# Attention and MLP on one core: both dense layers in seven products, shared PSUM bank pairs, a list that places every operation

## The chip, the cores and the metric

The kernel runs on one core of one Trainium2 chip. The metric is the device time in microseconds (us); lower is better. The core has a matrix engine (TensorE, PE in the profile, with PEld for its weight loads), VectorE (DVE), ScalarE (ACT), GpSimd (POOL) and SyncE (SP), which only starts transfers. Each engine works through its own queue in order; semaphores make one wait for another. Matmuls write to PSUM, eight banks of 512 fp32 values per partition.

## The reference

```python
scores = q @ k^T / sqrt(64)              # q, k, v: 8 batches x 12 heads x 448 x 64
attn   = maximum(scores, 0)**2 / 448
x      = heads of (attn @ v) side by side    # 3584 tokens x 768
h      = x @ w_in                        # 768 x 2048
g      = h * sigmoid(1.702 * h)
out    = g @ w_out                       # 2048 x 768
```

Inputs and output are fp32.

## The kernel before

**Units of attention.** Four heads of one batch are a unit, 24 in all. Its k and q are loaded, cast to fp16 and transposed: units 0 to 5 on PE (`trans_pe`, L138, with a copy on DVE, L142), the others by transposing transfers on SP's queue (`trans`, L111). A slot `s` is one seventh of a unit's scores: four 64x64 matmuls (L159) into a pair of PSUM banks, a ReLU on ACT (L175) or DVE (L173), and a square `x` on DVE (L447) into an `at` tile. When seven slots are squared, `a` multiplies them with v (28 matmuls, L190), and `xt_evac` (L210, L213) moves the result to a tile of x, transposed, with tokens in the free dimension.

**Groups of tokens.** The tokens are cut into eight groups of 384 and 512 in turn. Layer one, `m1` (L238): for each of 16 blocks of 128 hidden features, six matmuls of the whole group into one bank, GELU on ACT to an fp32 tile `gf` (L243), and a scaling ("widening") to fp16 on POOL into `gt` (L245). Layer two for group 0 and one odd piece: `m2` (L264), 16 matmuls per 128 tokens and half of the outputs.

**Seven products in layer two.** For the other groups, two 128-token pieces, two halves of the hidden features and two halves of the outputs form 2x2 blocks, and `pair` (L303) computes seven products of eight matmuls in place of eight. Sums of `gt` (L298) and of `w_out` (L288) are made on DVE. Each product has its own bank; DVE adds it, times 1/SC, to one or two places of the output tile `osb` (L314), after two of them were copied to `ea` and `eb` on ACT (L312). A piece without a partner goes through `single` (L389). Finished tiles are stored on SP's queue (L255); the last product of all is split into two halves of 192 columns with a store each.

**PSUM.** `ps_s` holds three pairs of banks for scores and attention results, `ps_m` two single banks for layers one and two.

**What sets the order.** A list of words, written out by hand or by a planner, is executed in order (`for w in words`). Each engine receives its instructions in the order of the words. A slot's ReLU is issued with its matmuls, or, with the letter h, after the next word of the dense layers (`release`). A few zero matmuls (`z`) and doubled slots (letter t) keep PE at work near the start.

Of the kernel before, what the change touches and what calls it, by code (L numbers as in the profile page):

```python
# [15 lines left out]
def kernel(  # L16
# [15 lines left out]
    NU = B * NP  # L32
    NK = DM // 128
    NF = DFF // 128
    NOUT = DM // 2
    SC = float(D * S)
    WQ = 4
    WO = 8

# [3 lines left out]
    for n in gblk:  # L43
# [3 lines left out]
    cst = ctx.enter_context(tc.tile_pool(name="cst", bufs=1))  # L47
    stp = ctx.enter_context(tc.tile_pool(name="stp", bufs=2))
    c16 = ctx.enter_context(tc.tile_pool(name="c16", bufs=3))
    v16p = ctx.enter_context(tc.tile_pool(name="v16p", bufs=5))  # L50
    qkT = ctx.enter_context(tc.tile_pool(name="qkT", bufs=3))
    rlp = ctx.enter_context(tc.tile_pool(name="rlp", bufs=3))
    atp = ctx.enter_context(tc.tile_pool(name="atp", bufs=11))
    xtp = ctx.enter_context(tc.tile_pool(name="xtp", bufs=3))
    gfp = ctx.enter_context(tc.tile_pool(name="gfp", bufs=3))
    gtp = ctx.enter_context(tc.tile_pool(name="gtp", bufs=1))
    smp = ctx.enter_context(tc.tile_pool(name="smp", bufs=1))
    osp = ctx.enter_context(tc.tile_pool(name="osp", bufs=3))
    ps_s = ctx.enter_context(tc.tile_pool(name="ps_s", bufs=3, space=bass.MemoryType.PSUM))
    ps_m = ctx.enter_context(tc.tile_pool(name="ps_m", bufs=2, space=bass.MemoryType.PSUM))  # L60

    ident = cst.tile([128, 128], F16, name="ident")
    gate = cst.tile([1, 64], F16, name="gate")
    warm = cst.tile([1, 1], F32, name="warm")
    win = [cst.tile([128, NK, WQ * 128], F16, name=f"win{i}") for i in range(NF // WQ)]
    wout = [[cst.tile([128, WO, NOUT], F16, name=f"wout{h}_{i}") for i in range(NF // WO)]
            for h in range(2)]

    wsum = [cst.tile([128, WO, NOUT], F16, name=f"wsum{i}") for i in range(3)]


    units = {}

    def quad(t, b, pr):
        return t[b].rearrange("(a i s) (p j) d -> i (s p) a (j d)", a=2, i=NP, j=J)[pr]

    def load_qk(u):
        b, pr = divmod(u, NP)
        st = units.setdefault(u, {})
        for n, t in (("k", k), ("q", q)):  # L80
            x = stp.tile([128, 2, S], F32, name=f"{n}st", tag=f"{n}st")
            nc.sync.dma_start(
                out=x,
                in_=quad(t, b, pr))
            st[n] = x

    def load_v(u):
        b, pr = divmod(u, NP)
        st = units.setdefault(u, {})
        x = v16p.tile([128, 2, S], F16, name="v16", tag="v16")  # L90
        nc.gpsimd.dma_start(
            out=x,
            in_=quad(v, b, pr))
        st["v16"] = x

    def cast(u, n, eng):
        st = units[u]
        c = c16.tile([128, J, 2, D], F16, name=f"{n}16", tag=f"{n}16")
        o = c.rearrange("p j a d -> p a j d")
        i = st[n].rearrange("p a (j d) -> p a j d", d=D)  # L100
        if eng is nc.scalar:
            eng.activation(out=o, in_=i, func=AF.Copy)
        else:
            eng.tensor_copy(out=o, in_=i)  # L104
        st[n + "16"] = c

    def trans(u):
        st = units[u]
        for n in ("k", "q"):
            t = qkT.tile([128, J, 128], F16, name=f"{n}T", tag=f"{n}T")  # L110
            nc.sync.dma_start_transpose(  # L111
                out=t[:, :, :], in_=st[n + "16"].rearrange("p j a d -> p (j a d)"))
            st[n + "T"] = t

    def load16(u, n):
        b, pr = divmod(u, NP)
        st = units.setdefault(u, {})
        x = c16.tile([128, 2, J, D], F16, name=f"{n}16", tag=f"{n}16")
        nc.gpsimd.dma_start(
            out=x,  # L120
            in_=quad({"k": k, "q": q}[n], b, pr))
        st[n + "16"] = x

    def cast16(u, n, eng):
        c = c16.tile([128, 2, J, D], F16, name=f"{n}16", tag=f"{n}16")
        o, i = c.rearrange("p a j d -> p a (j d)"), units[u][n]
        if eng is nc.scalar:
            eng.activation(out=o, in_=i, func=AF.Copy)
        else:
            eng.tensor_copy(out=o, in_=i)  # L130
        units[u][n + "16"] = c

    def trans_pe(u, n):
        st = units[u]
        ps = ps_m.tile([128, 1024], F16, name="tr", tag="mm")
        for j in range(J):
            for a in range(2):
                nc.tensor.matmul(  # L138
                    out=ps[64 * a:64 * a + 64, j * 128:(j + 1) * 128],
                    lhsT=st[n + "16"][:, a, j, :], rhs=ident[:, :], is_transpose=True)  # L140
        t = qkT.tile([128, J, 128], F16, name=f"{n}T", tag=f"{n}T")
        nc.vector.tensor_copy(out=t, in_=ps[:, 0:J * 128])  # L142
        st[n + "T"] = t

    early = []

    def scores(u, j, times=1, banks=False):
        st = units[u]
        if early:
            sc = early.pop()  # L150
        elif banks:
            sc = [ps_m.tile([128, 512], F32, name="scm", tag="mm") for _ in range(2)]
        else:
            sc = ps_s.tile([128, 2, 512], F32, name="sc", tag="sc")
        for s in [0, 1] * times:
            for a in range(2):
                r = slice(64 * a, 64 * a + 64)
                c = slice(64 * s, 64 * s + 64)
                nc.tensor.matmul(  # L159
                    out=sc[a][c, 0:S] if isinstance(sc, list) else sc[c, a, 0:S],  # L160
                    lhsT=st["kT"][r, j, c],
                    rhs=st["qT"][r, :, c],
                    start=True, stop=True)
        return sc

    def relu2(u, j, sc, dve=False):
        rl = rlp.tile([128, 2, S], F16, name="rl", tag="rl")
        at = atp.tile([128, 2, S], F16, name="at", tag="at")
        halves = [(rl, sc[:, :, 0:S])] if not isinstance(sc, list) else [
            (rl[:, a, :], sc[a][:, 0:S]) for a in range(2)]  # L170
        for o, i in halves:
            if dve:
                nc.vector.tensor_scalar(out=o, in0=i, scalar1=0.0, scalar2=None, op0=ALU.max)  # L173
            else:
                nc.scalar.activation(out=o, in_=i, func=AF.Relu)  # L175
        pend[u, j] = (at, rl)
        return at

    pend = {}

    def av_mm(u, j, at):
        st = units[u]
        if "av" not in st:
            av = ps_s.tile([128, 2, 512], F32, name="av", tag="sc")
            st["av"] = [av[:, 0, :], av[:, 1, :]]
            st["pair"] = av
        for s in range(2):
            for a in range(2):
                r = slice(64 * s, 64 * s + 64)
                nc.tensor.matmul(  # L190
                    out=st["av"][s][64 * a:64 * a + 64, 0:S],
                    lhsT=st["v16"][r, a, 64 * j:64 * j + 64],
                    rhs=at[r, a, :],
                    start=(j == 0), stop=(j == J - 1))
# [3 lines left out]
    def xt_evac(u):  # L198
        b, pr = divmod(u, NP)
        st = units[u]  # L200
        lo = b * J
        while lo < (b + 1) * J:
            g = max(i for i in range(NG) if gcum[i] <= lo)
            hi = min((b + 1) * J, gcum[g + 1])
            if g not in xts:
                xts[g] = xtp.tile([128, NK, 512], F16, name="xt", tag="xt")
            c = slice(64 * (lo - gcum[g]), 64 * (hi - gcum[g]))
            f = slice(64 * (lo - b * J), 64 * (hi - b * J))
            if "pair" in st:
                nc.vector.tensor_copy(out=xts[g][:, 2 * pr:2 * pr + 2, c], in_=st["pair"][:, :, f])  # L210
            else:
                for s in range(2):
                    nc.vector.tensor_copy(out=xts[g][:, 2 * pr + s, c], in_=st["av"][s][:, f])  # L213
            lo = hi
        st.pop("pair", None)
        st.pop("av", None)

    ats = {}

    held = []  # L220

    def release():
        while held:
            u, j, sc = held.pop()
            ats[u, j] = relu2(u, j, sc)


    gts = {}

    def m1(g, f):  # L230
        n = 64 * gblk[g]
        if f == 0:
            gts[g] = gtp.tile([128, NF, 512], F16, name="gt", tag=f"gt{g % 2}")
# [24 lines left out]
    def m2(g, m, h):  # L258
# [13 lines left out]
        if h == 1:  # L272
            store(g, m, 0, DM, (nc.sync, nc.sync))
# [291 lines left out]
```

## Time and profile before

| | |
|---|---|
| median of 3 runs | 381.79 us (381.56 to 382.59) |
| span of the profiled execution | 380.2 us |
| PE busy | 369.7 us, 3136 matmuls |
| DVE busy | 256.8 us, 426 instructions |
| ACT busy | 215.7 us, 315 instructions |
| POOL busy | 133.2 us, 198 instructions |
| granted TensorE clock | 0.998 |

The profile is of one execution; its span, from the first to the last instruction, lies 1.6 us under the median of the runs. Busy is the time in which at least one instruction of the engine was under way. A row of the profile names the line, the engine, the operation, output and input tile with their shapes, a count, and then the busy time and the mean length of one; what follows is the idle time before these instructions and who ended it. Instructions of one engine can overlap by their start and end, so a length can exceed the distance from one start to the next.

### The profile page before, as it was taken

What the parts mean: (1) busy time and instruction counts of PE and PEld (TensorE: products, weight loads), DVE (VectorE), ACT (ScalarE), POOL (GpSimd) and SP (SyncE); (2) the same over time, 40 slices, a digit from 0 to 9 for tenths busy, and PEclk for the clock granted to TensorE, in tenths of its full rate; (3) what the DMA queues carried; (4) which work ended last, traced back from release to release, by engine and by line L of the source; (5) the groups of instructions that cost most, each with busy time, mean ns of one, the idle gap of its engine ahead of it and who ended that gap; (6) DMA issues with size and microseconds to landing.
All of it is one profiled execution on the core that took longest, in us unless ns stands there. A gap on an engine that the chain in (4) does not pass through costs nothing.

```text
span 380.2 us, 7870 instructions
## 1 busy us (share of the span) xinstructions
PE 369.7 (97%) x3136; PEld 194.1 (51%) x3136; DVE 256.8 (68%) x426; ACT 215.7 (57%) x315; POOL 133.2 (35%) x198
## 2 busy tenths in 40 slices
PE   7889999999999999999999999999999999999993
PEld 3455554544555555544455555544555555454552
DVE  3999843689869977577874995484348795032673
ACT  3988854567766845565877546386556643323110
POOL 7543644432363243143246132232631213313000
PEclk9999999999999999999999999999999999999999
DMA  8999998977775977789569656580292303010333
GB/s 179 203 205 205 203 282 187 213 198 155 216 158 93 197 177 127 148 242 141 91 230 177 132 100 129 156 153 3 46 149 34 84 2 84 2 41 0 85 83 84
DMA packets 65221, 51.30 MB, mean 135 GB/s; under 512 B 35744, under 2 KB 61728, under 8 KB 65184
## 3 DMA queue, kind: packets, MB, share of 16 engines
q1 hardware_dynamic: 48416, 36.61, 39.8%
q0 software_dynamic: 16608, 14.09, 26.0%
q8 instruction: 24, 0.39, 0.4%
q10 hardware_dynamic: 160, 0.10, 0.1%
q14 instruction: 13, 0.11, 0.1%
HBM read 45.61 MB, written 11.01 MB: 149 GB/s over the span
## 4 chain that ended last, share of the span: by engine, by line
PE 90%; DVE 6%; issue 1%; ACT 1%; ACTq 0%
PE ht L238 39%; PE op L303 29%; PE sc L159 9%; PE av L190 7%; PE op L264 4%; DVE at L447 2%; DVE osb L314 1%; PE zp L422 1%; ACT rl L175 1%; PE tr L138 1%; DVE kT L142 1%; DVE xt L213 1%; DVE qT L142 0%; DVE rl L173 0%; ACT eb L312 0%
## 5 line engine op out<-in xcount | busy, mean ns | idle before, releaser
L238 PE MATMUL ht<-xt,win 128*128 128x384 f16 (+1 forms) x768 | 156.2, 353 | 0.0
L245 POOL TENSOR_SCALAR gt<-gf 128x384 f16<-128x384 f32 (+1 forms) x128 | 81.5, 637 | 195.9 <-ACT gf L243 190.7
L175 ACT ACTIVATE rl<-sc 128x896 f16<-128x896 f32 x144 | 126.3, 918 | 33.8 <-PE sc L159 29.0
L243 ACT ACTIVATE gf<-ht 128x384 f32<-128x384 f32 (+1 forms) x128 | 69.9, 546 | 89.2 <-PE ht L238 75.3
L447 DVE TENSOR_TENSOR at<-rl 128x896 f16<-128x896 f16 x168 | 104.8, 656 | 14.8 <-ACT rl L175 13.9
L238 PEld LDWEIGHTS <-win 128*128 128x128 f16 x768 | 72.7, 98 | 73.1 <-issue 10.3
L303 PEld LDWEIGHTS <-gt 128*128 128x128 f16 x408 | 38.5, 98 | 30.0 <-issue 4.5
L159 PE MATMUL sc<-qT,kT 64*64 64x448 f16 x696 | 48.1, 357 | 1.5 <-ACT rl L175 0.8
L303 PEld LDWEIGHTS <-as 128*128 128x128 f16 x312 | 29.9, 98 | 22.7 <-issue 2.7
L303 PE MATMUL op<-wout,as 128*128 128x384 f16 x224 | 40.5, 326 | 0.0
L303 PE MATMUL op<-wsum,gt 128*128 128x384 f16 x224 | 40.1, 326 | 0.0
L314 DVE SCALAR_TENSOR_TENSOR osb<-op,osb 128x384 f32<-128x384 f32 (+1 forms) x45 | 23.6, 544 | 21.2 <-PE op L303 20.8
L190 PE MATMUL av<-at,v 64*64 64x448 f16 x616 | 33.2, 350 | 0.1
L303 PE MATMUL op<-wout,gt 128*128 128x384 f16 (+1 forms) x184 | 32.4, 319 | 0.5 <-DVE osb L314 0.5
L210 DVE CAST xt<-av 128x896 f16<-128x896 f32 (+2 forms) x32 | 24.6, 793 | 9.3 <-PE av L190 9.2
L159 PEld LDWEIGHTS <-kT 64*64 64x64 f16 x696 | 17.4, 105 | 25.3 <-issue 18.3
L173 DVE TENSOR_SCALAR rl<-sc 128x896 f16<-128x896 f32 x24 | 26.0, 1087 | 4.6 <-PE sc L159 4.5
L298 DVE TENSOR_TENSOR as<-gt 128x1024 f16<-128x1024 f16 x36 | 24.2, 699 | 6.7 <-POOL gt L245 6.7
L190 PEld LDWEIGHTS <-v 64*64 64x64 f16 x672 | 19.7, 107 | 13.4 <-issue 2.8
L104 POOL CAST q<-qst 128x896 f16<-128x896 f32 x18 | 17.1, 948 | 11.3 <-DMA qst<-in_q_dram 10.5
L314 DVE SCALAR_TENSOR_TENSOR osb<-op,ea 128x384 f32<-128x384 f32 x22 | 12.1, 552 | 12.1 <-PE op L303 6.0
L314 DVE SCALAR_TENSOR_TENSOR osb<-op,eb 128x384 f32<-128x384 f32 x22 | 12.1, 551 | 11.7 <-PE op L303 11.7
(40 smaller groups left out, 178.1 us busy)
## 6 DMA issues: line engine op xcount, KB each, us to landing
out_dram<-osb SPq DMA_DIRECT2D x54, 192.0 KB, 2.7
kst<-in_k_dram SPq DMA_DIRECT2D x19, 448.0 KB, 4.9
qst<-in_q_dram SPq DMA_DIRECT2D x19, 448.0 KB, 5.6
v<-in_v_dram POOLq DMA_DIRECT2D x24, 224.0 KB, 4.9
win<-in_moe_w_in_dram POOLq DMA_DIRECT2D x8, 384.0 KB, 12.3
wout<-in_moe_w_out_dram POOLq DMA_DIRECT2D x4, 768.0 KB, 10.7
k<-in_k_dram POOLq DMA_DIRECT2D x5, 224.0 KB, 8.8
q<-in_q_dram POOLq DMA_DIRECT2D x5, 224.0 KB, 9.1
```

The source lines that it names most:

```text
L159: nc.tensor.matmul(out=sc[a][c, 0:S] if isinstance(sc, list) else sc[c, a, 0:S], lhsT=st["kT"][r, j, c], rhs=st["qT"][r, :, c], start=True ...
L173: nc.vector.tensor_scalar(out=o, in0=i, scalar1=0.0, scalar2=None, op0=ALU.max)
L175: nc.scalar.activation(out=o, in_=i, func=AF.Relu)
L190: nc.tensor.matmul(out=st["av"][s][64 * a:64 * a + 64, 0:S], lhsT=st["v16"][r, a, 64 * j:64 * j + 64], rhs=at[r, a, :], start=(j == 0), st ...
L210: nc.vector.tensor_copy(out=xts[g][:, 2 * pr:2 * pr + 2, c], in_=st["pair"][:, :, f])
L238: nc.tensor.matmul(out=ht[:, 0:n], lhsT=w[:, kk, fo:fo + 128], rhs=xts[g][:, kk, 0:n], start=(kk == 0), stop=(kk == NK - 1))
L243: nc.scalar.activation(out=gf[:, 0:n], in_=ht[:, 0:n], func=AF.Gelu_apprx_sigmoid, scale=1.0 / SC)
L245: nc.gpsimd.tensor_scalar(out=gts[g][:, f, 0:n], in0=gf[:, 0:n], scalar1=SC, scalar2=1.0, op0=ALU.mult, op1=ALU.mult)
L298: nc.vector.tensor_tensor(out=out_, in0=x, in1=y, op=op)
L303: nc.tensor.matmul(out=op[:, 0:cw], lhsT=lhs[:, f, :], rhs=w[:, f, c0:c0 + cw], start=(start and f == 0), stop=(stop and f == HF - 1))
L314: nc.vector.scalar_tensor_tensor(out=o, in0=op[:, 0:w], scalar=sc, in1=add, op0=ALU.mult, op1=ALU.add)
L447: nc.vector.tensor_tensor(out=at, in0=rl, in1=rl, op=ALU.mult)
```

## The change

Layer one gets seven products too. For groups 1 to 7, four blocks of hidden features times two halves of the model dimension times two halves of the tokens form 2x2 blocks; four units of seven products replace 16 blocks of six matmuls. A product is six matmuls (three of the model dimension, two of the features) of half a group, 256 or 192 columns. Sums of x (`t_sum`) are made per group on DVE, sums of `w_in` (`s_sum`) once.

Both layers now use the form of seven products in which intermediate results are chained: products 0, 2, 4 and 5 accumulate in bank 0 of a pair, 1 in bank 1, then 3 and 6 in bank 1. Between them, bank 0 is copied out (a "snapshot", on ACT or DVE), and bank 1 is added to a snapshot on DVE. In layer one these are `unit_snap` (t) and `unit_add` (b) on fp32 tiles `gf`, followed by GELU (g) and widening (v); in layer two `pair_snap` (h) and `pair_last` (l) on the output tile.

PSUM is four pairs of banks, P0 to P3, used by all stages; the word names the pair (`@2`). Each operation is a word of its own: matmuls of a slot `s`, ReLU `r`, square `x`, transfer `e` of attention results, casts `K` and `Q`, transposing transfers `Rk` and `Rq`, loads `Lk` and `Lq`, products `u` and `p`. A letter after a colon names the engine (a ACT, d DVE, p POOL). 45 of the 168 squares are on POOL, and seven of the casts of later units on DVE. Staging tiles of k and q have one buffer each (two before), `at` eight (eleven before), `gf` five (three before). The doubled slots, the zero matmuls among the slots and the split of the last product are gone. Group 0 and the pieces without a partner keep eight products.

```diff
-    stp = ctx.enter_context(tc.tile_pool(name="stp", bufs=2))
...
-    ps_s = ctx.enter_context(tc.tile_pool(name="ps_s", bufs=3, space=bass.MemoryType.PSUM))
-    ps_m = ctx.enter_context(tc.tile_pool(name="ps_m", bufs=2, space=bass.MemoryType.PSUM))
+    for name, bufs in (("cst", 1), ("kst", 1), ("qst", 1), ("k16", 2), ("q16", 2), ("v16", 4),
+                       ("kT", 3), ("qT", 3), ("rl", 3), ("at", 8), ("xe", 1), ("xo", 2),
+                       ("T1", 1), ("T2", 1), ("T4", 1), ("ge", 1), ("go", 1), ("gf", 5),
+                       ("asm", 2), ("osb", 3)):
+        pool(name, bufs)
+    for i in range(4):
+        pool(f"P{i}", 1, space=bass.MemoryType.PSUM)
...
+    def square(e, p, u, j):
+        rl = slots[u, j]
+        at = new("at", [128, 2, S], F16)
+        tt(at, rl, rl, ALU.mult, e)
+        slots[u, j] = at
...
+    def s_sum(e, p, i, n):
+        s1, s2, s4 = winS[i]
+        a11, a12, a21, a22 = (w_in_block(i, f, h) for f in range(2) for h in range(2))
+        o, x, y, op = {1: (s1, a21, a22, ALU.add), 2: (s2, s1, a11, ALU.subtract),
+                       3: (a21, a21, a11, ALU.subtract), 4: (s4, a12, s2, ALU.subtract)}[n]
+        tt(o, x, y, op, e)
...
+    def t_sum(e, p, g, n):
+        b11, b12, b21, b22 = (x_block(g, h, t) for h in range(2) for t in range(2))
+        if n == 3:
+            tt(b12, b12, b22, ALU.subtract, e)
+            return
+        x, y = {1: lambda: (b12, b11), 2: lambda: (b22, xsum[g, 1]),
+                4: lambda: (b21, xsum[g, 2])}[n]()
+        xsum[g, n] = new(f"T{n}", [128, HK, 256], F16)[:, :, 0:32 * gblk[g]]
+        tt(xsum[g, n], x, y, ALU.subtract, e)
...
+    def unit_product(e, p, g, i, n):
+        hn = 32 * gblk[g]
+        if n == 0:
+            hp[g, i] = pair(p, name="hx")
+        bank = (0, 1, 0, 1, 0, 0, 1)[n]
...
+        for t in range(2):
+            mm(hp[g, i][:, bank, t * hn:(t + 1) * hn],
+               lambda j: a[:, j, t * 128:(t + 1) * 128], lambda j: b[:, j, :], HK,
+               n in (0, 1, 3) and t == 0)
...
+    def unit_snap(e, p, g, i, n):
+        gfs[g, i, n] = new("gf", [128, 512], F32)
+        copy(e, half_of(gfs[g, i, n], g), half_of(hp[g, i][:, 0, :], g))
...
+    def unit_add(e, p, g, i, n):
+        t = half_of(gfs[g, i, unit_tile[n]], g)
+        tt(t, half_of(hp[g, i][:, 1, :], g), t, ALU.add)
...
+    def unit_widen(e, p, g, i, n):
+        fh, th = unit_place[n]
+        hn = 32 * gblk[g]
+        f = WQ * i + 2 * fh
+        widen(e, gt_of(g)[:, f:f + 2, th * hn:(th + 1) * hn],
+              half_of(gfs.pop((g, i, unit_tile[n])), g).rearrange("p (t c) -> p t c", t=2))
...
+    def pair_product(e, p, g, m, n):
+        if n == 0:
+            op[g, m] = pair(p, name="ox")
+        bank = (0, 1, 0, 1, 0, 0, 1)[n]
...
+    def pair_snap(e, p, g, m, n):
+        i, c = {0: (0, lo), 2: (0, hi), 4: (1, hi)}[n]
+        copy(e, out_tile(g, m + i)[:, c], op[g, m][:, 0, 0:NOUT], 1.0 / SC)
+
+    def pair_last(e, p, g, m, n):
+        i, c = {1: (0, lo), 3: (1, hi), 5: (1, lo), 6: (0, hi)}[n]
+        o = out_tile(g, m + i)[:, c]
+        if n == 5:
+            copy(e, o, op[g, m][:, 0, 0:NOUT], 1.0 / SC)
+        else:
+            nc.vector.scalar_tensor_tensor(out=o, in0=op[g, m][:, 1, 0:NOUT], scalar=1.0 / SC,
+                                           in1=o, op0=ALU.mult, op1=ALU.add)
...
+            "Q0:a jk1 jk2 V0 I tq0@0 eq0 tk1@1 jq2 K0:d tk0@2 ek1 tk2@3 ek0 s0.3@0 ek2 s0.0@1 jq1 "
...
+            "p6.0.5 l6.0.3 T7.1 T7.2 l6.0.5:d o5.2 T7.3 u7.1.0@1 t7.1.0:d u7.0.0@2 t7.0.0 u7.0.1 "
+            "b7.0.1 u7.1.1 b7.1.1 T7.4 g7.0.1 v7.0.1 u7.0.2 t7.0.2 p6.0.6 l6.0.6 o6.0 u7.0.3 "
...
```

## The prediction

> **What bounds the kernel now.** I read the page first: busy shares, then the chain that ended last.
>
> ```profile
> span 380.2 us, 7870 instructions
> PE 369.7 (97%) x3136; PEld 194.1 (51%) x3136; DVE 256.8 (68%) x426; ACT 215.7 (57%) x315; POOL 133.2 (35%) x198
> PE 90%; DVE 6%; issue 1%; ACT 1%; ACTq 0%
> ```
>
> PE is busy 97% of the span and carries 90% of the chain. Busy is not yet paced work, so I took paces from unbroken runs. In the chain in order of time (start, length, what):
>
> ```profile
> 341.04 6.51 PE ht L238 x30
> ...
> 351.44 6.51 PE op L303 x40
> ```
>
> 30 matmuls of 512 columns in 6.51 us are 217 ns (the 6-long pieces of 1.29 give 215), and 40 of 384 are 162.5 ns. For short ones the timeline of PE near the end has
>
> ```profile
> 372.60 0.82 PE L303 MATMUL op<-wout,gt 128*128 128x192 f16 x8
> ```
>
> 8 of 192 columns: 0.82 less the last one's own 0.24 is seven steps of 82 ns. So a matmul costs columns/2.4 + 2 to 2.5 ns, and 192 columns still hide their weight loads. Other pieces of the chain give 12 score matmuls in 0.69 us (57 ns each, 0.23 per slot) and 28 attention-value ones in 1.32.
>
> Paced work before: layer one 384 x 215 + 384 x 162.5 = 145.0 us; layer two 808 x 162.5 (16 half-wide ones as 8) = 131.3; 174 slots 40.0; values 31.6; transposes 5.4; warming 4.4; zeros 1.3. Sum 359. PE works from 1.2 to 374.7, so 14 us are stalls: about 8 before 40 us, 7 from there to 358, 2 at the end. The windows by stage (length, then busy us of PE, weight loads, DVE, ACT, POOL) show which engine holds the early part:
>
> ```profile
> 10.00:20.00 10.00, 9.03 (x148) 4.89 (x151) 9.95 (x22) 9.75 (x12) 5.70 (x10) 1.00 1.26 203
> 20.00:30.00 10.00, 9.12 (x154) 5.13 (x146) 9.85 (x20) 8.65 (x11) 4.01 (x6) 1.00 1.25 205
> 100.00:125.00 25.00, 25.00 (x212) 13.97 (x208) 21.44 (x37) 16.27 (x25) 10.74 (x14) 1.00 0.62 132
> ```
>
> DVE sets the first 30 us at 99%; later PE is full and DVE stands at 48 to 86%. PE's work is the term to count, and DVE the engine to watch.
>
> DVE's occupancy is less than its instructions' length. In the timeline
>
> ```profile
> 11.66 1.15 DVE L447 TENSOR_TENSOR at<-rl 128x896 f16<-128x896 f16 x2
> ```
>
> two squares of 0.618 take 1.15, so a queued one costs 0.54. Likewise two osb updates of 0.55 take 1.03 (0.47 to 0.48 each). Costs below are such start-to-start ones: ReLU on DVE 1.01, sums of 1024 elements 0.60, of 768 0.47, PSUM rows of 384 0.47 and, with 128 elements more at 1.0 ns (the 192- and 384-wide updates, 0.358 and 0.551, give that slope), of 512 0.60; on ACT ReLU 0.80, 384 elements 0.39, 512 0.49.
>
> **What the Trainium skill says.** "TensorE: Matmul & The Clock Gate", section "Back-to-back issue gap", prices an isolated matmul at N/2.4 + 2.5 ns, and streams with weight loads at 131 ns for N=512. The trace agrees with the first (162.5, 215) and not with the second. So 256 columns are 109 ns. "SBUF — State Buffer", section "Who interferes with whom": a DVE instruction with two SBUF inputs contends with a GpSimd instruction that reads SBUF, and the second to issue blocks until the first is done. The trace agrees:
>
> ```profile
> 139.52 0.93 POOL L104 CAST q<-qst 128x896 f16<-128x896 f32 x1
> 139.84 1.09 DVE L447 TENSOR_TENSOR at<-rl 128x896 f16<-128x896 f16 x1
> ```
>
> The square starts inside the cast and lasts 1.09 in place of 0.618. Eight of the 18 casts hold a DVE sum so, 4.5 us in all, 0.25 a cast. "GPSIMD Engine Reference", section 3.1 on elementwise cycle accounting, gives a two-input add of 2048 fp32 elements 4.50 us, about 2.6 cycles an element. No row here shows one; scaled to 896 it is an estimate of 2.0 us.
>
> **The change, part by part.**
>
> Layer one on PE. Seven of eight groups become four units of seven products of six matmuls at half width: 672 x 109 + 504 x 82 = 73.2 + 41.3; group 0 stays, 96 x 162.5 = 15.6. Together 130.1 against 145.0: -15. The ideal eighth would be more; the 2 ns a matmul and group 0 take the rest.
>
> Layer two on PE: 704 in pairs and singles and 96 plain, 808 before with the halves: no change. The same seven products only combine inside PSUM. Six doubled slots go (24 x 57 = 1.4) and six zero matmuls (1.3). PE's sum is 341.3, 18 less.
>
> DVE. Removed: 45 squares go to POOL (-24), the three-term combinations (89 updates and 12 plain evacuations, -48) become 33 updates and 19 copies (+25). Added: 84 additions of a bank to a snapshot (48 x 0.60 + 36 x 0.47 = +46), 34 snapshots (+19), 28 sums of tokens (+12), 16 of w_in (+7.5), five ReLUs (+5), seven casts (+5). Fewer sums of gt and w_out (-8). Net about +39: 277 us of paced work where a like count of before gives about 240. ACT gains 50 snapshots and 37 scaled copies, loses 22 copies, 10 casts and 5 ReLUs: +15, to 211. POOL: 45 squares of 2.0 make it about 216, with 112 widenings in place of 128. Neither is full, and each works behind PE. Behind a square on POOL stand casts, v's loads and widenings; a late widening keeps one of the five gf tiles, and then the next snapshot has nowhere to go and product 2 waits. A unit uses four gf tiles, so this cover is thin; it is part of the allowance for stalls.
>
> Waits in the shared banks. Product 2 may enter bank 0 only after the snapshot of product 0; product 3 may start bank 1 only after the addition that reads product 1. A snapshot comes 0.27 + 0.50 us after its product's last matmul starts draining, and a product is 0.65 (or 0.49) long, so one product of another unit between covers it; the list interleaves two units nearly everywhere. I walked the last group, where no attention fills gaps: from the end of the last values, DVE has transfer, two sums, one update, the third sum, a snapshot and the first addition done near 5 us; PE reaches the product that needs it after 6. Covered. If the snapshot's engine lags by its queue, PE waits with all behind it; that is the allowance below.
>
> Moved loads: the same transfers, but one staging buffer for k and q each (two before) on SP's queue, behind transposes and stores. Landing is 4.9 and 5.6 us, a unit takes some 14 us, so one buffer suffices; cover gone, a late cast costs up to 5 us on the engine that casts, seven times DVE. I take zero to 5 and zero.
>
> Start: k of unit 0 is now cast behind q's transfer on DVE, so the first ReLU comes near 10.3 instead of 8.9; DVE is continuous from about 7.2. The end: the last product is no longer split, 1.30 in place of 0.66 plus a wider update and store; 5.5 us after the last matmul become about 6.2.
>
> Sums by stage of the list (PE / DVE, us): up to the first unit of group 1 46.4 / 49.5; from there to group 7 250.8 / 208.4; after 39.7 / 19.5. In twelve stretches of the middle, DVE exceeds PE unaided only after group 1 (15.6 against 14.0). Holds: ordinary ones 3% (10 us of before's DVE time). For the squares on POOL the bounds are 0.25 each, as a cast, and 0.86: sums come every 1.4 us or so, so a 2.0 us square meets one three times in four and holds it 1.15. I take 0.5. With it the larger of the two engines, stretch by stretch, adds to 349.4; plus 7.2 at the start and 6.2 at the end 362.8. Stalls: before lost 2% in the middle with DVE slack; with DVE near 90% I take 4%, 10 us, and 1.5 at the end: 374.3. The median of the runs is 1.6 above the profiled span (381.8 against 380.2): 376.
>
> **Rivals.**
> 1. The squares on POOL hold DVE at the full 0.86. For: the casts' holds grow from 0.04 (widenings) to 0.25 with the length. DVE then exceeds PE in five stretches (27.8 against 23.5 after group 5, 29.7 against 27.6 after group 6, 55.3 against 46.4 at the start), the larger-engine sum is 357.5, and both engines full cost 6% of the middle, as the 10 to 30 us windows show PE losing to a full DVE: 357.5 + 13.4 + 15 + 1.5 + 1.6 = 389. It ends slower than before from a hold of about 0.65 each. Against: holds count only where DVE leads.
> 2. No hold to speak of and before's own 2%: 341.5 + 13.4 + 7 + 1.5 + 1.6 = 365. For: before's list keeps PE at 98% from 40 us. Against: DVE never was this full there.
> 3. PE waits in the banks: 28 units x 0.6 us more gives 393. For: five such waits a unit, four pairs for everything. Against: the walk above.
> 4. Gain spent, within 0.3% (380.6 to 382.9, about what a measurement can tell from none): holds near 0.65.
>
> **How the numbers follow.** Main case 0.37 (369 to 380), rival 2 0.18, rival 1 0.26, rival 3 0.10, rival 4 0.09. Faster 0.55, same 0.09, slower 0.36. The range runs from rival 2's middle to a little over rival 3, 366 to 396; the main case alone 369 to 380.
>
> **What would show it.** Right: paces of 82 and 109 ns in the unit rows; PE paced work 341; DVE 290 to 310 busy; first unit of group 1 near 60 us. Wrong: squares on POOL well over 2 us with DVE sums stretched beside them (rival 1); PE idle released by snapshots and additions (rival 3); short matmuls paced by weight loads above 95 ns, which would take back 504 x 13 = 7 us; DVE waiting for k or q from DMA.

## The result: a quarter slower

The changed kernel takes 475.44 us (471.70 to 476.28), the kernel before 381.68 (381.47 to 382.59): a ratio of 1.243, with a 95% interval of 1.238 to 1.248. The forecast was 376, with a range up to 396. The profiled execution has a span of 469.8 us.

The page of the changed kernel, the lines that answer to the first fence of the prediction: span, engines, chain.

```profile
span 469.8 us, 8978 instructions
...
PE 380.5 (81%) x3602; PEld 242.5 (52%) x3602; DVE 326.4 (69%) x487; ACT 234.6 (50%) x365; POOL 216.4 (46%) x246
...
PE 51%; DVE 25%; ACT 11%; issue 6%; DMA 4%; POOL 2%; SPq 0%; POOLq 0%; DVEq 0%; ACTq 0%
```

PE fell from 97% busy to 81%, and its share of the chain that ended last from 90% to 51%. Over the whole span no engine took its place: DVE is idle for 143 us, ACT for 235, POOL for 253. A program without a full engine waits for its own dependences. The windows, as in the prediction (length, then busy us of PE, weight loads, DVE, ACT and POOL, then granted clock, DMA share and GB/s), say that PE falls short all along and not in one stage. In the third of them DVE is at 96%, so it may lead there:

```profile
10.00:20.00 10.00, 7.93 (x131) 4.73 (x131) 8.96 (x14) 7.50 (x9) 8.43 (x11) 1.00 1.19 226
20.00:30.00 10.00, 7.09 (x110) 4.01 (x104) 8.40 (x16) 7.43 (x10) 4.30 (x7) 0.83 1.24 199
100.00:125.00 25.00, 20.99 (x229) 12.07 (x229) 24.03 (x35) 18.77 (x27) 12.34 (x13) 1.00 0.54 125
```

The paces of the half-wide products are as forecast. Two runs of them in the timeline of PE:

```profile
305.77 1.47 PE L200 MATMUL hx<-xo,win 128*128 128x256 f16 x12
350.35 1.65 PE L200 MATMUL hx<-xe,win 128*128 128x192 f16 x18
```

Twelve of 256 columns are eleven steps of 109 ns and 0.27 for the last one, eighteen of 192 are seventeen steps of 82 ns and 0.25. With these paces all products of the execution add to about 339 us (before: 357). From the first product to the last, what is left beside that sum is what I call PE's stalls: 124 us, against 17 in the kernel before. All of the loss is there. The stalls take in products that ran at a lower granted clock. The share of the clock that was not granted, times the span, bounds this part: at most 12 us of the 124 (an estimate from the mean clock of 0.975).

Who waits for whom among the dense products and what reads them, from the waits of the changed kernel (us in total, times, longest):

```profile
ACT gf L211 <- DVE gf L88: 38.7, 29, 4.4
...
DVE gf L88 <- ACT gf L79: 23.2, 20, 2.2
PE ox L200 <- DVE osb L385: 18.3, 11, 5.0
PE hx L200 <- DVE gf L88: 16.8, 26, 1.5
```

They are the snapshots, additions and GELUs of layer one's units and the updates of layer two, handing over to each other. The chain in order of time (start, length, what) shows the form of it in the first unit of group 4:

```profile
239.01 0.57 DVE gf L88
239.58 0.02 issue
239.60 0.50 ACT gf L79
240.10 0.04 issue
240.14 1.66 PE hx L200 x18
```

An addition, then a snapshot, then products, each beginning 0.02 to 0.05 us after the one before has ended. But the addition reads bank 1 of the pair and the snapshot reads bank 0; nothing in the arithmetic puts one behind the other.

### The profile page after: what moved, and what is told of

It reads as the page before. It is cut to its first block, busy times and chain, and to the rows that moved or that the text cites. A ratio compares the mean times of both kernels' runs of the same rounds, so it can differ in the third digit from the quotient of the medians.

```text
span 469.8 us, 8978 instructions
## 1 busy us (share of the span) xinstructions
PE 380.5 (81%) x3602; PEld 242.5 (52%) x3602; DVE 326.4 (69%) x487; ACT 234.6 (50%) x365; POOL 216.4 (46%) x246
## 4 chain that ended last, share of the span: by engine, by line
PE 51%; DVE 25%; ACT 11%; issue 6%; DMA 4%; POOL 2%; SPq 0%; POOLq 0%; DVEq 0%; ACTq 0%
PE ox L200 18%; PE hx L200 16%; DVE gf L88 6%; DVE at L88 5%; PE av L178 5%; PE sc L150 4%; PE ht L200 3%; ACT gf L211 3%; ACT gf L79 3%; ACT rl L161 3%; DVE gf L83 3%; DMA q<-in_q_dram 2%; DVE rl L158 2%; PE os L200 2%; DVE osb L385 2%
## 5 line engine op out<-in xcount | busy, mean ns | idle before, releaser
L88 POOL TENSOR_TENSOR at<-rl 128x896 f16<-128x896 f16 x45 | 79.3, 1764 | 60.5 <-ACT rl L161 47.4
L88 DVE TENSOR_TENSOR gf<-hx,gf 128x512 f32<-128x512 f32 (+1 forms) x84 | 52.3, 631 | 46.2 <-ACT gf L79 23.2
L214 POOL TENSOR_SCALAR go<-gf 128x512 f16<-128x512 f32 x64 | 43.3, 677 | 81.3 <-ACT gf L211 78.7
L214 POOL TENSOR_SCALAR ge<-gf 128x384 f16<-128x384 f32 x64 | 37.0, 578 | 58.2 <-ACT gf L211 55.3
L200 PEld LDWEIGHTS <-winS 128*128 128x128 f16 x504 | 46.7, 98 | 31.9 <-issue 26.6
L211 ACT ACTIVATE gf<-gf 128x512 f32<-128x512 f32 (+1 forms) x84 | 47.1, 580 | 20.7 <-DVE gf L88 19.9
L200 PE MATMUL hx<-T,winS 128*128 128x256 f16 (+1 forms) x336 | 41.7, 265 | 14.6 <-DVE gf L88 7.4
L200 PE MATMUL ox<-wout,go 128*128 128x384 f16 x256 | 48.7, 339 | 3.7 <-ACT osb L81 2.1
L200 PE MATMUL ox<-wT,asm 128*128 128x384 f16 x176 | 32.4, 327 | 13.3 <-DVE osb L385 10.3
L200 PE MATMUL hx<-xo,win 128*128 128x256 f16 x288 | 37.5, 275 | 4.1 <-DVE gf L83 2.8
```

What stands on the lines that cost most here:

```text
L88: eng[e].tensor_tensor(out=o, in0=x, in1=y, op=op)
L200: nc.tensor.matmul(out=o, lhsT=lhs(i), rhs=rhs(i), start=start and i == 0, stop=i == n - 1, skip_group_check=True)
L211: nc.scalar.activation(out=o, in_=i, func=AF.Gelu_apprx_sigmoid, scale=1.0 / SC)
L214: eng[e].tensor_scalar(out=o, in0=i, scalar1=SC, scalar2=1.0, op0=ALU.mult, op1=ALU.mult)
```

## Experiments

Stalls of PE are counted as above in each run's profile. "Before" was run again beside each; it stayed at 381.4 to 382.6.

| kernel | us, median (range) | ratio to before, 95% interval | PE's paced work | its stalls |
|---|---|---|---|---|
| before | 381.7 (381.5 to 382.6) | | 357 | 17 |
| changed | 475.4 (471.7 to 476.3) | 1.243 (1.238, 1.248) | 339 | 124 |
| e1 squares on DVE | 466.8 (466.0 to 467.5) | 1.219 (1.213, 1.226) | 339 | 118 |
| e2 no snapshots | 449.4 (447.8 to 450.9) | 1.174 (1.163, 1.184) | 339 | 103 |
| e3 both layers plain | 455.8 (453.2 to 458.4) | 1.191 (1.174, 1.208) | 368 | 79 |
| e4 layer two plain | 479.3 (479.2 to 479.4) | 1.252 (1.247, 1.257) | 354 | 116 |
| e5 halves | 481.6 (479.8 to 483.6) | 1.262 (1.258, 1.267) | 339 | 134 |
| e6 banks apart | 408.1 (405.5 to 410.6) | 1.069 (1.064, 1.075) | 339 | 63 |
| e7 and squares on DVE | 400.5 (399.8 to 401.1) | 1.049 (1.046, 1.052) | 339 | 53 |
| e8 new order throughout | 440.7 (439.6 to 442.4) | 1.154 (1.150, 1.157) | 339 | 93 |
| e9 e6, new order from 68 us | 408.8 (407.2 to 411.6) | 1.071 (1.066, 1.076) | 339 | 64 |
| e10 e7, new order from 68 us | 396.1 (394.1 to 396.9) | 1.035 (1.032, 1.039) | 339 | 49 |
| e11 plain, banks apart | 440.5 (438.8 to 441.8) | 1.153 (1.148, 1.158) | 368 | 63 |
| e12 before, two banks as one tile | 541.5 (540.4 to 543.1) | 1.419 (1.414, 1.423) | 357 | 179 |
| e13 e7 without snapshots | 394.2 (393.8 to 394.8) | 1.032 (1.029, 1.035) | 339 | 46 |

Some of them leave out work. e2 and e13 leave out the snapshots and additions of layer one, so that its combination is incomplete. e3, e4 and e11 leave out sums of w_out that the six single pieces still need, so those pieces use unsummed weights. e8's order put in-place sums of the weights ahead of plain products of group 0 that read the unsummed ones. Their times are read with that in mind. e1 to e4 have two runs each, the others four or six.

### One part at a time: squares, snapshots, layers

e1 puts the 45 squares back on DVE:

```diff
-s1.1@0 tk3@2 ek3 r1.1 r1.0 x0.5:p jwa3 V2 x1.0
+s1.1@0 tk3@2 ek3 r1.1 r1.0 x0.5 jwa3 V2 x1.0
```

> The changed kernel (475 us) with all 45 squares of GpSimd moved back to VectorE, at the same places of the list; the result is the same. If the holds of VectorE by squares on GpSimd are the cause (rival 1), VectorE loses about 22 us of held time for 24 us of work, but the 1.8 us squares leave the path and PE's waits shrink by 25 us or more: below 450. If PE waits for the links of the chains in the shared banks (rival 3), whoever squares, it stays between 465 and 485.

It gained 8.7 us, and lies where rival 3 had it. The squares on POOL do hold DVE. The groups of the changed kernel:

```profile
L88 DVE TENSOR_TENSOR at<-rl 128x896 f16<-128x896 f16 x123 | 95.8, 799 | 11.3 <-ACT rl L161 9.0 <-PE av L178 1.5
L88 POOL TENSOR_TENSOR at<-rl 128x896 f16<-128x896 f16 x45 | 79.3, 1764 | 60.5 <-ACT rl L161 47.4 <-PE av L178 5.4 <-issue 4.0
```

A square on DVE takes 799 ns there in the mean, 670 in e1. All two-input SBUF and bank operations of DVE (its TENSOR_TENSOR rows, lengths added) last 227.5 us in the changed kernel and 232.9 in e1; the 45 squares that e1 adds are 45 x 0.67 = 30.2 of that, so the holds were 227.5 - 202.7 = 24.8 us, 0.55 a square. But DVE has 143 us of idle time. The edit takes away the holds and the longer squares together and puts 30 us of work back on DVE; all this comes to 8.7 us.

e2 takes the snapshots and additions of layer one away; GELU reads bank 1 itself:

```diff
     def unit_add(e, p, g, i, n):
-        t = half_of(gfs[g, i, unit_tile[n]], g)
-        tt(t, half_of(hp[g, i][:, 1, :], g), t, ALU.add)
+        gfs[g, i, unit_tile[n]] = new("gf", [128, 512], F32)
+        gelu(half_of(gfs[g, i, unit_tile[n]], g), half_of(hp[g, i][:, 1, :], g))
```

> The changed kernel without the chain's links in layer one: no snapshots (50 on ACT, 34 on DVE) and no additions (84 on DVE); GELU reads bank 1 directly where the addition stood. It leaves out that part of the computation. PE's products are unchanged. If the links of layer one cost PE's waits (about 40 us before layer-one products), 425 to 440. If holds by GpSimd or the list as a whole are at fault, PE's waits move elsewhere and it stays above 455.

It gained 26 us and ended between its two forecasts; 103 us of stalls stayed. e3 and e4 put plain products in the places of the chained ones, in the same list with the same four pairs: for layer two the words p, h, l and A become m and n, for layer one u, t, b and T become f and g.

```diff
-u1.0.0@2 Rq6 u1.0.1 u1.1.0@1 t1.0.0 T1.1 T1.3 T1.2 u1.0.2 t1.0.2 W1.1 Lq8
+f1.0@2 Rq6 f1.1 f1.4@1 Lq8
```

> The changed kernel's list, pools and four bank pairs, but eight products in both layers: plain products of six and sixteen matmuls at the places of the seven, each evacuated once; no sums of x, w_in, w_out or gt but those of single pieces. PE's paced work is 15 us more in layer one and 14 us more in layer two, about 372. If the chains are the cause, stalls fall from 130 to under 40 us and it ends at 395 to 415, in spite of more work. If the list with four shared pairs is at fault, stalls stay near 100 us and it ends above 450.

> The changed kernel with layer one as it is and layer two plain (eight products, two evacuations per piece, no sums of w_out, no sums of gt but those of single pieces). PE has 14 us more work. If the chains cause the waits, the 41 us before products of layer two fall to under 15: 445 to 455. If only layer one's chain or the holds matter, 480 to 490.

Neither came near what would have shown the chains alone as the cause. With plain products in both layers, and DVE 40% busy, PE's stalls fall by 45 us, but 79 stay; plain products in layer two alone gain no time. So seven products, and DVE, are not enough to explain it. Something that plain and chained products share in the changed kernel makes PE stand: the order of the list, or the four pairs.

### The pair waits as one

Then I went through the trace operation by operation, and asked of each start which earlier end lies just ahead of it. For most kinds of operation it is the engine's last instruction, an input, or a buffer's last reader. For snapshots, additions, GELUs and products of a unit it often was none of these, but the access to the same pair that stands before it in the list, in whichever bank. In the timeline of the changed kernel, unit 0 of group 4 (columns: start, length, engine, what, idle time before it and what ended it):

```profile
236.19 0.66 PE L200 MATMUL hx<-xe,win 128*128 128x192 f16 x6
...
236.89 0.49 ACT L79 ACTIVATE gf<-hx 128x384 f32<-128x384 f32 x1 [0.97 <-PE hx L200]
...
237.43 0.66 PE L200 MATMUL hx<-xe,win 128*128 128x192 f16 x6 [0.27 <-ACT gf L79]
...
239.01 0.56 DVE L88 TENSOR_TENSOR gf<-hx,gf 128x384 f32<-128x384 f32 x1 [0.22 <-PE hx L200]
...
239.60 0.49 ACT L79 ACTIVATE gf<-hx 128x384 f32<-128x384 f32 x1 [2.23 <-DVE gf L88]
...
240.14 0.66 PE L200 MATMUL hx<-T,winS 128*128 128x192 f16 x6 [0.75 <-ACT gf L79]
```

The first product goes to bank 0 and is read by the snapshot at 236.89. The second goes to bank 1, which nobody holds; it starts at 237.43, 0.05 us after the snapshot of bank 0 has ended. The addition at 239.01 reads bank 1, and the snapshot at 239.60, of bank 0, starts 0.03 us after it, although both only read. Product 3, into bank 1, needs that addition (ended 239.57) and starts 0.05 us after the snapshot of bank 0 (240.09). When every access to a pair is put behind the one before it in the list, such starts are explained; with waits by bank, they are not. In the 28 units of layer one there are 159 places where an access follows, in the list, another engine's access to the other bank of its pair. In the trace of the changed kernel none of the 159 begins before the earlier one has ended, and 103 begin within 0.1 us after it. 45 of the places are a read behind a read.

e5 and e6 test it. To make the banks separate tiles, the operations that read both banks at once (ReLU and the transfer of values) must be cut in two; e5 does that alone, and is the control. e6 has one thing more: a pair is two tiles of one bank, and `Two` hands out the bank that is asked for. The first lines of the diff are e5's change, those from the pool on are e6's:

```diff
+        for b in range(2):
+            ...
+                nc.scalar.activation(out=rl[:, b, :], in_=sc[:, b, 0:S], func=AF.Relu)
...
-        pool(f"P{i}", 1, space=bass.MemoryType.PSUM)
+        for b in range(2):
+            pool(f"P{i}{b}", 1, space=bass.MemoryType.PSUM)
...
     def pair(p, dt=F32, name="pp"):
-        return new(f"P{p}", [128, 2, 512 if dt is F32 else 1024], dt, name)
+        return Two([new(f"P{p}{b}", [128, 512 if dt is F32 else 1024], dt, name)
+                    for b in range(2 if dt is F32 else 1)])
```

> The control of the next run: the changed kernel, but the ReLU of a slot and the transfer of attention values are done bank by bank, two half-wide instructions for each. On ACT 139 slots then take 2 x 0.44 us in place of 0.80 (+11 us), on DVE 29 slots +1.5 us and 36 transfers +2 us. Nothing else changes, the two banks of a pair are still one tile. Both theories: 470 to 490 us, at most a few per cent from the changed kernel's 475.

> The run before with one thing more: each of the four pairs is two tiles of one bank, so that the program orders accesses by bank and not by pair. The list of operations, their engines and the banks they use are the same. Theory A (in the trace of the changed kernel every access to a pair waits for the access to that pair before it in the list, whichever bank it is in, reads after reads too: product 2 in bank 0 starts 0.05 us after the addition that reads bank 1, a GELU that reads bank 0 0.09 us after such an addition): the waits by bank are all that is left, a walk through the list with the trace's durations gives about 60 us less than with waits by pair, so 400 to 425 us, the waits before unit and layer-two products falling from 86 us to under 35. Theory B (the order of the list, or too few pairs for all stages, makes PE wait): within 2% of the run before.

Both ended inside what theory A expects. e6 is 73.5 us faster than its control, at the same list, engines and banks. (Up to 10 us of this can be the granted clock: 0.962 over 480.3 us and 0.981 over 408.8 leave 18 and 8 us that were not granted. This is an estimate.) The same place of the list in e6's timeline:

```profile
216.94 0.66 PE L211 MATMUL hx<-xe,win 128*128 128x192 f16 x6
...
217.63 0.49 ACT L80 ACTIVATE gf<-hx 128x384 f32<-128x384 f32 x1 [0.87 <-PE hx L211]
...
217.84 0.67 PE L211 MATMUL hx<-xe,win 128*128 128x192 f16 x6
...
219.65 0.55 DVE L89 TENSOR_TENSOR gf<-hx,gf 128x384 f32<-128x384 f32 x1
...
219.89 0.49 ACT L80 ACTIVATE gf<-hx 128x384 f32<-128x384 f32 x1 [1.77 <-PE hx L211]
...
220.25 0.66 PE L211 MATMUL hx<-T,winS 128*128 128x192 f16 x6
```

The second product now starts while ACT still reads bank 0 (217.63 to 218.12), the snapshot at 219.89 runs beside the addition, and product 3 starts 0.05 us after that addition, with ACT still in the other bank. Of the 159 places, 105 now begin before the earlier access has ended, 18 of the 45 reads behind reads among them; in e5 it is none. The waits of PE for the units' additions and for layer two's updates are nearly gone (16.8 and 18.3 us in the changed kernel):

```profile
PE ox L211 <- DVE osb L396: 1.6, 3, 1.0
...
PE hx L211 <- DVE gf L89: 0.2, 1, 0.2
```

PE's idle time ahead of the products of units and of layer two's pairs adds up to 61 us in e5 and 8 in e6, so some 53 of the 73.5 us stand before the chained products; the rest belongs to other uses of the pairs and to the clock. The split also lets each bank go to its next user by itself, where a pair went with its last reader; no run takes this apart from the order inside the pair.

e12 makes the same edit the other way in the kernel before, whose dense products take two tiles of one bank in turn. There the two become one tile, with nothing else changed:

```diff
-    ps_m = ctx.enter_context(tc.tile_pool(name="ps_m", bufs=2, space=bass.MemoryType.PSUM))
+    ps_m = ctx.enter_context(tc.tile_pool(name="ps_m", bufs=1, space=bass.MemoryType.PSUM))
+    mm_pair = ps_m.tile([128, 2, 512], F32, name="mm", tag="mm")
...
-        ht = ps_m.tile([128, 512], F32, name="ht", tag="mm")
+        ht = mm_bank()
```

`mm_bank` gives the two banks of that one tile in turn.

> The kernel before, unchanged but for one thing: the two banks that its dense products, transposes and first slots take in turn are one tile of two banks, and not two tiles. Theory A (accesses to one tile go in the program's order, whichever bank they are in): each of some 223 products can start only when the evacuation of the product before it is done, about 0.2 us of draining, 0.5 to 0.6 of reading and 0.05 to PE: 0.8 us each, 178 us less what slots, values and stalls between them cover; 480 to 560 us. Rival (the waits by pair come from how the changed kernel uses its pairs, and not from the tile): within 1% of 381.

It takes 541.5 us, inside the forecast of 480 to 560. From its page, and a product in its timeline:

```profile
span 540.6 us, 7889 instructions
...
PE 397.7 (74%) x3136; PEld 194.7 (36%) x3136; DVE 253.5 (47%) x426; ACT 218.0 (40%) x315; POOL 126.7 (23%) x198
```

```profile
345.89 0.60 ACT L250 ACTIVATE gf<-mm 128x512 f32<-128x512 f32 x1
...
346.54 1.46 PE L245 MATMUL mm<-xt,win 128*128 128x512 f16 x6 [0.75 <-ACT gf L250]
```

The product at 346.54 goes into the other bank than the one that the GELU reads until 346.49. The same banks, as two tiles, cost 381. One tile stays in use throughout here, so this is the order inside a tile alone.

### What is left: 400 against 381

e7 takes e1's edit in the kernel with the banks apart.

> The run before with the 45 squares of POOL on DVE. With the banks apart PE is nearer to full, so the squares' waits[...] and their length of 1.7 us on POOL should count more or less as before: the same walk gives 12 us less than with the squares on POOL (theory A and B alike), 385 to 415 us if theory A holds for the run before. If it ends under 380.6 us, the changed kernel's arithmetic does pay once its waits are gone; if it stays above 383, the order of the list takes the rest.

It gives 7.7 us, as in the paired banks. e11 is e3 with the banks apart:

> The changed kernel with plain products in both layers (the run with both layers plain, 455.8 us: eight products, no sums but those of the single pieces, the sums of w_out that the single pieces need left out) and with the banks apart and the ReLU in halves. PE's paced work is 368 us. Theory A (the waits by pair were what made even the plain products slow in the changed frame): 405 to 425 us, PE's stalls falling from 79 us to 35 to 50. Rival (the list made the plain products slow): not under 440 us.

The expected 405 to 425 missed, at 440.5, just inside what its rival, the list, expects (not under 440). Its stalls are 63 us, those of e6. So with the banks apart the seven products cost PE no stalls over plain ones, and their 29 us of paced work show in full: 440.5 to 408.1. Of e3's 79 us of stalls the edit took 16, or some 26 if the halves cost here what they cost in e5 (stalls of 134 against 124: an estimate); the other 63 come with the frame, that is the list, its start, the buffers and the work beside the products.

e8, e9 and e10 try the order of the list; e8 also moves work between engines (72 squares on POOL in place of 45). A walk through the program, with the traces' durations and the waits by bank, took for each engine the operation that was ready and stood first in the list. Around the first unit of group 3, in e9 (the third number of an r is the half):

```diff
-p2.0.0@3 e11.0 T3.1 l1.2.6 T3.2 T3.3 u3.0.0@1 u3.0.1 u3.1.0@2 t3.0.0 b3.0.1
+V15 T3.1 r11.0.0 o1.3 x11.6 r11.0.1 u3.0.0@0 x11.3:p r11.4.0:d u3.2.0@2
```

> The same operations on banks that wait singly (as in the run with the banks apart), in another order: a walk through the program with the durations of the traces lets each engine take, of the operations whose inputs and buffers are there, the one that stands first in the changed kernel's list, and small changes of that rank and of the engine (ACT, DVE or POOL) of ReLU halves, squares, snapshots, casts and transfers were kept where the walk's end came earlier. For the list with the banks apart the walk gave 396 us against 408.1 measured, for the same with squares on DVE 385 against 400.5; for the new order it gives 365 to 369. Theory C (the order of the list takes the rest between 400 us and the kernel before): 374 to 384 us, PE's stalls falling from 62 us to 25 to 35. Theory D (the chained products and the few buffers make PE wait in whatever order): not under 396 us.

> The kernel with the banks apart (408.1 us), every operation on the engine it has there, the first 68 us of the list as they are, and from there on another order: each engine takes, of the operations whose inputs and buffers are there, the one that stands first in the list, in a walk with the traces' durations. Most of PE's operations move by a few places, at most by 42. The walk gave 396 us for the list against 408.1 measured and gives 368 for this order. Theory C (the order of the list takes the rest): 376 to 388 us, PE's stalls falling from 62 us to 30 to 40. Theory D (the chained products and the few buffers make PE wait in whatever order): not under 400 us.

> The same, made for the kernel with the banks apart and all squares on DVE (400.5 us); the walk gave 385 us for the list against 400.5 measured and gives 365 for this order. Theory C: 373 to 384 us, with a good half of that range faster than the kernel before; theory D: not under 392 us.

All three missed what theory C expects and ended where theory D had them. e8 moved the start too and lost most there: it is 5 us of paced work behind e6 by 40 us and 19 by 80, and its chain up to 64.6 us is mostly loads of q, of w_in and of w_out. Its mean granted clock is also the lowest of all, 0.944. e9, with the first 68 us left alone, gained nothing and e10 4.3 us. The walk lacked something that an order fitted to it uses up: a step between 64-row products (scores and values) and dense ones costs 0.09 us each way, and e10's trace has 216 such steps where e7's has 130, 8 us more. So theory C is not shown: the order that I could make was no better than 4 us, and a better one was not found. Theory D has two parts. e11 speaks against the chained products; the few buffers stand untested, for no run changes their number.

e13 takes away e7's snapshots and additions, 65 us of DVE's work.

> The kernel with the banks apart and the squares on DVE (400.5 us), without the snapshots and additions of layer one (GELU reads the banks themselves; that part of the combination is left out). DVE loses some 65 of its 332 us, ACT some 15. Theory E (DVE's queue makes PE wait): PE's stalls fall from 54 us to 25 to 35 and the time to 372 to 382. Theory F (the order of the list and its start make PE wait): stalls of 45 or more, 391 us or more. In the paired banks the same edit took 26 us.

6 us came back and 46 us of stalls stayed, as theory F has it, so DVE's queue is not most of what holds PE there. What can be placed: by 40 us PE has done 20.9 us of paced work in e7 and 30.3 in the kernel before, 9.4 us of the 36 that e7 stalls more. In e7's chain in order of time, two loads of w_in fill most of that start:

```profile
11.27 10.90 DMA win<-in_moe_w_in_dram
22.45 13.90 DMA win<-in_moe_w_in_dram
36.41 3.10 PE ht L211 x18
```

The first product of layer one starts at 36.41 there and at 28.11 in the kernel before, whose chain has no load in it. No run moves the loads alone, so this is where to look and not a cause shown. The rest of the 36 us lies in the middle, some 7 to 10 in each 100, and stays open. No version was found that beats the kernel before; the best, e10, takes 396.1.

## Why the prediction was wrong

**PE's work: right.** 341.3 us were counted, 339 are in the trace (the 704 products of layer two in pairs and singles are 712, which with the 96 plain ones are the same 808); 109 and 82 ns were the paces, as the Trainium skill's "TensorE: Matmul & The Clock Gate" ("Back-to-back issue gap") gave them. e6 against e11 shows that the saving is real: between seven products and plain ones in both layers it is 29 us of paced work and 32 us of time. Layer two's part is 15 (e4, with layer two plain, has 354 us), so layer one's is 14.

**"Waits in the shared banks": the step that failed.** It said that product 2 enters bank 0 after the snapshot of product 0, and product 3 bank 1 after the addition that reads product 1, and that "one product of another unit between covers it". That is a walk by bank, and by bank it nearly held, though its own figures are tight (0.77 us against a product of 0.65 or 0.49): in e6 PE idles 8 us before the chained products. But the program waits by tile, and a pair is one tile: product 1 waits for the snapshot, the snapshot of product 2 for the addition, reads for reads. A unit then is a single chain of products and evacuations, and one other unit between doesn't cover it: PE idles 59 us before these products in the changed kernel. The loss is 93.8 us, and 99.9 with the halves of e5; e6 takes 73.5 of that away, some 53 of it before the chained products. Rival 3 had the place right, but counted only waits by bank that lag by 0.6 us a unit, 17 us in all. The Trainium skill's "Perfetto Trace Analysis" ("Matmuls") asks for independent products to rotate through different banks, so that one is evacuated while the next runs. The changed kernel does so, and e12 shows that it is not enough in these programs: in the same two banks the overlap is lost when they are one tile.

It stands in the code and in the program's waits. In the code, `pair` makes one tile of two banks, while the kernel before took its dense products' banks as single tiles and read its two-bank score tiles whole. And of the 28 GELUs of a unit's product 5, which read bank 0 alone, 20 wait for DVE by the semaphores in the trace, 12 of them without waiting for PE: the addition that reads bank 1 stands ahead of them, and has waited for PE already. In e6 three wait for DVE.

**The squares: size nearly right.** The hold was taken as 0.5 us each and is 0.55; the square was estimated at 2.0 us from "GPSIMD Engine Reference" and takes 1.76 (1.68 when nothing is in its way). Put back, they give 8.7 us, so rival 1 was not the cause. Whether a hold counts only where DVE leads is not settled: DVE may lead in some stretches (it is 96% busy from 100 to 125 us), and no run takes the holds alone.

**"I take 4%": too small for another reason.** With the pairs and the squares out of the way, PE stalls 53 us where the sums allowed 26 (the 374.3 forecast less 1.2 ahead of the first product, 6.2 behind the last and 341.3 of work). The start was taken as before's with a first ReLU 1.4 us later; it came 2.3 us later, at 11.25, and by 40 us PE had done 20 us of work in place of 30. The first unit of group 1, forecast near 60 us, starts at 73. The middle was priced by how full the engines are, at 4%; e13, in which DVE has 65 us less to do, gives back only 6, so fullness was not the measure.

**DVE busy 290 to 310: low.** It is 326. The 277 us were start-to-start costs of queued operations; an operation that starts behind a wait takes its full length, 0.62 in place of 0.54 for a square. How much of the difference this is, no run shows. **Staging buffers at zero:** not refuted. The 4% of DMA in the chain are the first load of all (4.2 us), a load of q that doesn't go through them (9.5 from 14.28) and a store (2.7). **The end:** 6.2 us forecast, 5.6 measured from the last product to the end of the span.

## What to carry to other kernels

Before counting on one bank being read while its neighbour is written, ask what the program takes as the unit of waiting: in these kernels two banks that are one tile are one resource, for reads too, and a few lines of a timeline around one product show it. When PE, DVE and ACT are all under 85% over the span and the chain alternates between them in steps of 0.03 to 0.05 us, look for a wait that the arithmetic doesn't need before looking at counts of work. An order fitted to a model of an earlier trace loses what the model leaves out, so a gain of 20 us on paper is no gain until it has run.

## What the runs showed of the hardware

TensorE's granted clock fell in kernels where PE had long pauses: 0.998 in the mean before, 0.975 in the changed kernel, 0.962 in e5, 0.981 in e6, 0.993 in e7. It shows most at the end, where eight products of 384 columns that took 1.47 us elsewhere took 2.72:

```profile
458.52 2.72 PE L200 MATMUL ox<-wT,go 128*128 128x384 f16 x8 [5.05 <-DVE osb L385]
```

The pause before it was 5.05 us, and the clock record is at half from 456.99 us on. So the products after the pause took 1.25 us more; that the pause brought this about no run shows. Before this the changed kernel has four shorter stretches at half clock, 3.4 us each, and two of them begin 1.4 and 1.1 us after pauses of 2.5 and 3.2 us. e12 has the most stalls and 0.997: its pauses are many and short, and its one stretch at half clock before the end follows the longest of them, 2.2 us. So the sum of the pauses doesn't decide it. That their length does is not shown: a pause of 2.6 us in the changed kernel, at 162.8, was followed by no such stretch.

A change between products of 64 rows and columns of the array (scores and values) and dense ones costs PE 0.09 us at each step, though nothing is waited for. In both kernels a score product starts 256 ns after a dense one of 384 columns, where the next dense one starts after 162; in the changed kernel it is 202 against 109 ns for 256 columns. The kernels change about as often (126 and 130 times).
